# Keys of the second batch turned by a DMA transpose, and their copy moved ahead of two loads

## The chip, the cores and the metric

The kernel runs on one core of a Trainium2 chip. The metric is the device time of one launch in microseconds. A core has five engines that run their own instruction lists: TensorE (matrix multiplies), VectorE, ScalarE, GpSimd (POOL) and SyncE (SP). The last two also start most of the DMA transfers here, GpSimd the loads that change the type from float32 to bfloat16, SyncE the transposes within on-chip memory and the stores of the output. Sixteen DMA engines do the transfers of all queues.

## The reference, cut to what matters

Grouped attention over 8 batches (16 query heads share 4 key and value heads, 384 positions, head size 64), followed by a feed-forward block with a squared ReLU on all 3072 tokens:

```python
scores = scale * np.matmul(q, k.transpose(0, 1, 3, 2))
attn = np.exp(scores - max) ; attn = attn / sum(attn)
x = np.matmul(attn, v)            # heads side by side: 3072 x 1024
h = np.maximum(x @ w_in, 0.0)     # 3072 x 2048
out = h * h @ w_out               # 3072 x 1024, float32
```

Inputs are float32; the kernel computes in bfloat16 with float32 sums.

## The kernel before, in words

The kernel is written through a recorder (`Recorder`). Every operation is added with its engine, the tiles it reads and writes, and a modelled cost. The recorder keeps a modelled clock for each engine and a modelled end of the work in each DMA queue (`ring`), derives the semaphore waits from the reads and writes, and in the end gives each engine its list in the order of adding. Within one engine the order is thus fixed before the launch; a late transfer holds up everything behind the instruction that waits for it.

**Work of one batch.** Keys and queries must lie with the head size across partitions, so they are turned. The keys of a group are first written twice side by side (`dup_k`, line 263) so that two query heads can be scored at once. Then either TensorE turns them by a multiply with the identity into PSUM, from where VectorE copies them to `kT` (`turn_k_pe`, lines 291 and 297, one group of keys, three 128x128 blocks, per call), or one DMA transpose on SyncE's queue turns all four groups at once (`turn_k_dma`, line 272). Queries have the same two ways: `turn_q_pe` (lines 308 and 315, six blocks of one group) and `turn_q_dma` (line 278, half of a batch: two groups, twelve blocks). Scores, exponentials on ScalarE (line 344 for batch 0, 365 later), the multiply with the values (line 380) and the division (395) follow; the attention output is turned into `xT` on TensorE for batch 0 (line 413) and by DMA after that (line 400). The feed-forward block of a batch reads `xT`: sixteen column blocks of the up-projection (line 437, `w_in` in eight slices, two column blocks to a slice), then six output tiles of the down-projection (line 493, sixteen matmuls each, `w_out` in four quarters: two halves of the columns by two halves of the rows).

For batch 0 the down-projection goes through the first column half for its three row tiles, and then the second half the same way; within the first two tiles it does the upper half of the rows of `w_out` for both before the lower half for either.

**Order.** All weight loads, and the loads of batches 0 and 1, are added to GpSimd's list by hand before the planner starts. The planner is the long loop at the end. At each step it collects candidates (score bursts, value multiplies, turns, pieces of the feed-forward block), gives each the modelled time at which its inputs and a PSUM bank are there, and takes the most urgent of those that are ready, or the earliest. `turn_q` is the list of turns for TensorE in batches 0 and 1; a turn of batch 1 may go while fewer than six value pairs of batch 0 are done, or once all of batch 0's `xT` is there. `chores` holds work for GpSimd and SyncE, put into their lists when the planner's clock reaches the modelled end of what they read. From batch 2 on, `prepare` puts there the copy of the keys, one DMA turn for keys, two for queries, and the copy of the values. The loads of batch 2 are added when `turn_q` is empty. Modelled costs of a DMA turn are 1.4 for keys and 2.5 for half the queries, or 8.0 when the modelled load queue still has work at that time; in that case the load queue is made longer by the 1.4 or 2.5.

In the kernel before, batch 0 is turned on TensorE, and of batch 1 four groups of keys and two groups of queries; the other two groups of queries of batch 1 are turned by DMA.

Of the kernel before, what the change touches and what calls it, by code (L numbers as in the profile page):

```python
# [136 lines left out]
def bass_gqa_attention__then__ffn_squared_relu_kernel(  # L137
# [26 lines left out]
    def sb(name, shape, dt=bf16):  # L164
        return nc.alloc_sbuf_tensor(name, shape, dt)

    ident = sb("ident", [128, 128])
    q_st = [sb(f"q_st{i}", [128, H, NJ * D]) for i in range(NST)]
# [3 lines left out]
    k_dup = [sb(f"k_dup{i}", [128, NU, 2, D]) for i in range(2)]  # L172
# [54 lines left out]
    def load_v(b):  # L227
        st = b % NST
        R.add("gpsimd", lambda g: g.dma_start(  # L229
            v_st[st].ap().rearrange("p (g j) d -> p g (j d)", g=HKV),  # L230
            v[b].rearrange("g (p j) d -> p g (j d)", j=NJ)),
            writes=[("v_st", st)], dma=f"v{st}", cost=1.1, issue=0.8)

    def load_q(b, h0, h1):
        st = b % NST
        R.add("gpsimd", lambda g: g.dma_start(  # L236
            q_st[st][:, h0:h1, :],
            q[b, h0:h1].rearrange("h (p j) d -> p h (j d)", j=NJ)),
            writes=[("q_st", st, h // 4, h % 4 // 2) for h in range(h0, h1, 2)], dma=f"q{st}_{h0}",
            cost=0.265 * (h1 - h0), issue=0.8)  # L240
# [4 lines left out]
    def load_w_in(i):  # L245
        R.add("gpsimd", lambda g: g.dma_start(  # L246
            w_in_sb[:, :, i * WC:(i + 1) * WC],
            moe_w_in[:, i * WC:(i + 1) * WC].rearrange("(c p) f -> p c f", p=128)),
            writes=[("w_in", i)], dma=f"wi{i}", cost=2.65, issue=0.9)
# [9 lines left out]
    def dup_k(b, g0=0, g1=HKV):  # L259
        n = (g1 - g0) * NJ  # L260
        src = (k_st[b % NST] if b else k_f32)[:, g0 * NJ:g1 * NJ, :].unsqueeze(2).to_broadcast([128, n, 2, D])
        dst = k_dup[b % 2][:, g0 * NJ:g1 * NJ, :, :]
        R.add("gpsimd", lambda e: e.tensor_copy(dst, src),  # L263
              reads=[("k_st", b % NST) if b else ("k_f32", g) for g in range(g0, g1)],
              writes=[("k_dup", b % 2, g, x) for g in range(g0, g1) for x in range(2)], cost=0.125 * n)
# [5 lines left out]
    def turn_k_dma(b):  # L271
        R.add("sync", lambda e: e.dma_start_transpose(
            out=kT[b % 2].ap(), in_=k_dup[b % 2].ap().rearrange("p n x d -> p (n x d)")),
            reads=[("k_dup", b % 2, g, x) for g in range(HKV) for x in range(2)],
            writes=[("kT", b % 2, g) for g in range(HKV)], dma="turn_k", cost=1.4, shared=8.0)

    def turn_q_dma(b, half):
        R.add("sync", lambda e: e.dma_start_transpose(
            out=qT[b % 2][:, 12 * half:12 * half + 12, :],
            in_=q_st[b % NST][:, 8 * half:8 * half + 8, :].rearrange("p h e -> p (h e)")),  # L280
            reads=[("q_st", b % NST, 2 * half + i, x) for i in range(2) for x in range(2)],
            writes=[("qT", b % 2, 2 * half + i, t) for i in range(2) for t in range(6)], dma=f"turn_q{half}", cost=2.5, shared=8.0)
# [247 lines left out]
    aug_v(0, "gpsimd")  # L530
    load_q(1, 0, 8)
    load_q(1, 8, 16)
    load_w_in(1)
    load_v(1)
    dup_k(1)
    for i in range(2, 6):
        load_w_in(i)
    aug_v(1, "gpsimd")
# [36 lines left out]
    for group in ((0, 1), (2, 3), (4, 5), (6, 7), (8, 9), (10, 11)):  # L575
        if 0 < group[0] < NU - 2:
            smalls += [[(u, 0, 512)] for u in group] + [[(u, 512, 256) for u in group]]
        else:
            smalls += [[(u, c0, 384)] for c0 in (0, 384) for u in group]
    turn_q = [(0, 0, "a"), (0, 0, "c")]  # L580
    turn_q += [(b, g, w) for b in range(2) for g in range(HKV) for w in "kq"
               if (b, g) != (0, 0) and (b, g // 2, w) != (1, 1, "q")]
    sc_q = [(0, n) for n in range(len(smalls))] + [(b, u) for b in range(1, B) for u in range(0, NU, 2)]
    av_q = [(b, c) for b in range(B) for c in range(8)]
    o_q = []
# [1 line left out]
    scored, pairs, turned, up_done = set(), 0, 1, -1  # L587
    x_done = {b: 0 for b in range(B)}
    loaded, queued = 1, 1
    chores = [([("q_st", 1, 2, 0)], lambda: turn_q_dma(1, 1))]  # L590
    turned_g |= {(1, g, t) for g in (2, 3) for t in range(6)}

    def prepare(b):
# [20 lines left out]
    while av_q or av_open or sc_q or o_q or f_head is not None:  # L614
# [18 lines left out]
        if turn_q:  # L633
            b, g, w = turn_q[0]
# [5 lines left out]
        elif av_q:  # L640
            b, c = av_q[0]
# [5 lines left out]
        if sc_q:  # L647
            b, u = sc_q[0]
# [25 lines left out]
        if f_head is not None and not lanes:  # L674
            b, chunks, need, banks, piece = f_head
# [15 lines left out]
        if what[2] == "turn":  # L691
            b, g, w = turn_q.pop(0)
# [5 lines left out]
        elif what[2] == "av":  # L698
            b, c = av_q.pop(0)
            av_open = (b, c, av(b, c, spare))  # L700
            next(av_open[2])
        elif what[2] == "av2":
            b, c, rest = av_open
# [8 lines left out]
        elif what[2] == "o":  # L712
            b, c, _ = o_q.pop(0)
            turn_o_pe(b, c, spare)
            x_done[b] += 1
        elif what[2] == "sc":
            b, u = sc_q.pop(0)
# [44 lines left out]
```

## Time and profile before

| What | Value |
| --- | --- |
| Median of 3 runs (range) | 428.36 us (427.99 to 428.46) |
| Profiled execution: its own time | 427.99 us |
| Its span, first to last instruction | 426.2 us |
| Granted TensorE clock | 1.000 |
| TensorE busy | 419.3 us, 98% of the span |
| TensorE weight loads busy | 231.6 us, 54% |
| VectorE, ScalarE, GpSimd busy | 157.9, 194.7, 55.2 us |
| Moved by DMA | 44.30 MB, mean 104 GB/s |
| Loads started by GpSimd (q0) | 17.44 MB, 32.8% of 16 engines' span |
| Transposes, stores, first loads (q1) | 25.86 MB, 29.3% |

In the rows of the profile, "PE" is TensorE's matmuls, "PEld" its weight loads, "DVE" VectorE, "ACT" ScalarE, "POOL" GpSimd, "SP" SyncE; "POOLq" or "SPq" mark the issue of a transfer. A row of the order in time begins with the start and the length of a group of instructions in us, then engine, line, operation, the output and input tiles and the count; brackets give the time that the engine sat idle ahead of it and what ended that. The matmuls are pipelined and their ends are modelled, so the distances between weight loads say more about TensorE's pace than the matmuls' own durations.

### The profile page before, as it was taken

What the parts mean: (1) busy time and instruction counts of PE and PEld (TensorE: products, weight loads), DVE (VectorE), ACT (ScalarE), POOL (GpSimd) and SP (SyncE); (2) the same over time, 40 slices, a digit from 0 to 9 for tenths busy, and PEclk for the clock granted to TensorE, in tenths of its full rate; (3) what the DMA queues carried; (4) which work ended last, traced back from release to release, by engine and by line L of the source; (5) the groups of instructions that cost most, each with busy time, mean ns of one, the idle gap of its engine ahead of it and who ended that gap; (6) DMA issues with size and microseconds to landing.
All of it is one profiled execution on the core that took longest, in us unless ns stands there. A gap on an engine that the chain in (4) does not pass through costs nothing.

```text
span 426.2 us, 7806 instructions
## 1 busy us (share of the span) xinstructions
PE 419.3 (98%) x3433; PEld 231.6 (54%) x3463; DVE 157.9 (37%) x332; ACT 194.7 (46%) x194; POOL 55.2 (13%) x67
## 2 busy tenths in 40 slices
PE   8999999999999999999999999999999999999997
PEld 5565554565545655455554555545564465446544
DVE  3664431343424443234442344333441244114412
ACT  6957730576246772457735577731240033003300
POOL 8680001414012004004000000000000000000000
PEclk9999999999999999999999999999999999999999
DMA  9999999999699269549919310052001100110012
GB/s 179 192 175 200 186 202 204 225 155 170 103 192 163 31 131 126 123 98 145 105 52 173 88 45 18 2 107 94 25 2 49 74 26 1 51 74 26 1 67 82
DMA packets 96915, 44.30 MB, mean 104 GB/s; under 512 B 77296, under 2 KB 90864, under 8 KB 96880
## 3 DMA queue, kind: packets, MB, share of 16 engines
q0 software_dynamic: 36544, 17.44, 32.8%
q1 hardware_dynamic: 59664, 25.86, 29.3%
q8 instruction: 27, 0.44, 0.4%
q10 hardware_dynamic: 672, 0.49, 0.4%
q14 instruction: 8, 0.07, 0.1%
HBM read 35.65 MB, written 12.58 MB: 113 GB/s over the span
## 4 chain that ended last, share of the span: by engine, by line
PE 96%; POOL 2%; ACT 1%; issue 1%; DVE 0%; POOLq 0%
PE ps L437 40%; PE ps L493 39%; PE ps L380 8%; PE ps L355 7%; ACT expT L344 1%; PE ps L334 1%; POOL q_st L236 1%; PE ps L413 0%; POOL k_dup L263 0%; PE ps L291 0%; POOL w_in_sb L246 0%; POOL v_st L229 0%; POOL k_st L204 0%; PE ps L308 0%; DVE y_sb L502 0%
## 5 line engine op out<-in xcount | busy, mean ns | idle before, releaser
L437 PE MATMUL ps<-xT,w_in_sb 128*128 128x384 bf16 x1024 | 175.0, 326 | 0.0
L493 PE MATMUL ps<-w_out_sb,h2T 128*128 128x512 bf16 (+2 forms) x754 | 166.9, 375 | 2.2 <-issue 1.0
L365 ACT ACTIVATE expT<-ps 128x3072 bf16<-128x3072 f32 x42 | 114.5, 2726 | 63.2 <-PE ps L355 62.6
L437 PEld LDWEIGHTS ps<-xT,w_in_sb 128*128 128x128 bf16 x1024 | 97.1, 98 | 69.6 <-issue 6.2
L447 ACT ACTIVATE h2T<-hr 128x384 bf16<-128x384 f32 x128 | 64.5, 522 | 142.9 <-DVE hr L445 142.9
L493 PEld LDWEIGHTS ps<-w_out_sb,h2T 128*128 128x128 bf16 x784 | 73.7, 98 | 87.2 <-issue 5.1
L445 DVE TENSOR_SCALAR hr<-ps 128x384 f32<-128x384 f32 x128 | 71.3, 558 | 106.5 <-PE ps L437 106.5
L502 DVE COPY y_sb<-ps 128x512 f32<-128x512 f32 (+2 forms) x49 | 33.4, 681 | 123.9 <-PE ps L493 123.9
L380 PEld LDWEIGHTS ps<-v_aug,expT 128*128 128x128 bf16 x1152 | 40.0, 97 | 7.0 <-issue 0.6
L380 PE MATMUL ps<-v_aug,expT 128*128 128x65 bf16 x1152 | 41.9, 193 | 0.0
L395 DVE TENSOR_TENSOR o_sb<-ps,rinv 128x384 bf16<-128x384 f32 x64 | 35.7, 558 | 2.2
L355 PE MATMUL ps<-qT,kT 64*128 64x512 bf16 (+1 forms) x336 | 34.6, 325 | 0.0
L355 PEld LDWEIGHTS ps<-qT,kT 64*128 64x128 bf16 x336 | 13.0, 94 | 20.4 <-issue 6.1
L389 DVE RECIPROCAL rinv<-ps 128x6 f32<-128x6 f32 x64 | 12.2, 190 | 26.2 <-PE ps L380 26.1
L344 ACT ACTIVATE expT<-ps 128x1024 bf16<-128x1024 f32 (+1 forms) x20 | 17.1, 981 | 0.9 <-PE ps L334 0.9
L268 POOL COPY v_aug<-v_st 128x768 bf16<-128x768 bf16 x8 | 6.7, 833 | 83.0 <-PE ps L380 69.6
L263 POOL COPY k_dup<-k_st 128x1536 bf16<-128x1536 bf16 x7 | 10.3, 1469 | 43.1 <-DMA k_st<-in_k_dram 43.0
L236 POOL DMA_DIRECT2D q_st<-in_q_dram x17 | 14.9, 884 | 0.9 <-POOLq L747 0.8
L204 POOL DMA_DIRECT2D k_st<-in_k_dram x7 | 5.3, 760 | 39.2 <-DMA qT<-q_st 39.2
L334 PE MATMUL ps<-qT,kT 64*128 64x384 bf16 (+2 forms) x48 | 7.2, 331 | 0.4 <-DVE qT L315 0.2
L246 POOL DMA_DIRECT2D w_in_sb<-in_moe_w_in_dram x8 | 7.1, 894 | 0.0
L229 POOL DMA_DIRECT2D v_st<-in_v_dram x8 | 6.3, 785 | 0.1
(26 smaller groups left out, 41.0 us busy)
## 6 DMA issues: line engine op xcount, KB each, us to landing
out_dram<-y_sb SPq DMA_DIRECT2D x47, 256.0 KB, 2.0
q_st<-in_q_dram POOLq DMA_DIRECT2D x14, 384.0 KB, 8.9
w_in_sb<-in_moe_w_in_dram POOLq DMA_DIRECT2D x8, 512.0 KB, 15.1
w_out_sb<-in_moe_w_out_dram POOLq DMA_DIRECT2D x4, 1024.0 KB, 31.4
v_st<-in_v_dram POOLq DMA_DIRECT2D x8, 192.0 KB, 10.3
k_st<-in_k_dram POOLq DMA_DIRECT2D x7, 192.0 KB, 4.2
q_st<-in_q_dram POOLq DMA_DIRECT2D x3, 192.0 KB, 5.0
xT<-o_sb SPq DMA_TRANSPOSE x28, 3.0
```

What stands on the lines that cost most here:

```text
L236: R.add("gpsimd", lambda g: g.dma_start(q_st[st][:, h0:h1, :], q[b, h0:h1].rearrange("h (p j) d -> p h (j d)", j=NJ)), writes=[("q_st", st ...
L344: R.add("scalar", lambda e: e.activation(dst, src, AF.Exp, scale=0.125), reads=keys, writes=[("expT", (b * NU + u) % NEX, t) for u, _, _ i ...
L355: m = pe.matmul(flat[:, k0 * HC + c0:k0 * HC + c1], kT[b % 2][64 * x:64 * x + 64, u + k0, :], q_cols(b, (u + k0) // NJ, x, c0, c1))
L365: R.add("scalar", lambda e: e.activation(dst, src, AF.Exp, scale=0.125), reads=keys, writes=[("expT", (n + m) % NEX, t) for m in range(2) ...
L380: m = pe.matmul(po[:, f - 6 * s2, 0:D + 1], w, v_aug[b % 2][:, g * NJ + j, 0:D + 1], start=(j == 0), stop=(j == NJ - 1))
L389: R.add("vector", lambda e: e.reciprocal(rinv[r].ap().unsqueeze(2), po[:, :, D:D + 1]), reads=[("bank", i)], writes=[("rinv", r)], cost=0.13)
L395: R.add("vector", lambda e: e.tensor_tensor(dst, srcv, rbv, ALU.mult), reads=[("bank", i), ("rinv", r)], writes=[("o_sb", o, s2)], cost=0.48)
L437: m = pe.matmul(bank(i)[:, 0:S], w_in_sb[:, kc, c * 128:(c + 1) * 128], xT[b % NXT][:, kc, :], start=(kc == 0), stop=(kc == NKC - 1))
L445: R.add("vector", lambda e: e.tensor_scalar_max(hr[r][:, :], bank(i)[:, 0:S], 0.0), reads=[("bank", i)], writes=[("hr", r)], cost=0.48)
L447: R.add("scalar", lambda e: e.activation(h2T[b % 2][:, c, :], hr[r][:, :], AF.Square), reads=[("hr", r)], writes=[("h2T", b % 2, c)], cost ...
L493: m = pe.matmul(bank(i)[:, 0:n], h2T[b % 2][:, c, i3 * 128:(i3 + 1) * 128], w_out_sb[:, c, c0:c1], start=(c == 0), stop=(c == NFC - 1))
L502: R.add("vector", lambda e: e.tensor_copy(ysl, bank(i)[:, 0:n]), reads=[("bank", i)], writes=[("y", yb)], cost=0.08 + n / 960)
```

## The change

Two edits, both for batch 1. On GpSimd's hand-written list the copy of its keys (`dup_k(1)`) moves from behind the load of `w_in` slice 1 and the load of its values to a place ahead of both. And its four groups of keys leave TensorE's list of turns; instead a chore puts one DMA transpose of all four groups into SyncE's list, ahead of the DMA turn of half its queries. What stays in `turn_q` for batch 1 are the queries of groups 0 and 1.

```diff
     load_q(1, 0, 8)
     load_q(1, 8, 16)
+    dup_k(1)
     load_w_in(1)
     load_v(1)
-    dup_k(1)
     for i in range(2, 6):
         load_w_in(i)
     aug_v(1, "gpsimd")
...
     turn_q = [(0, 0, "a"), (0, 0, "c")]
     turn_q += [(b, g, w) for b in range(2) for g in range(HKV) for w in "kq"
-               if (b, g) != (0, 0) and (b, g // 2, w) != (1, 1, "q")]
+               if (b, g) != (0, 0) and (b == 0 or (g < 2 and w == "q"))]
...
-    chores = [([("q_st", 1, 2, 0)], lambda: turn_q_dma(1, 1))]
+    chores = [([("k_dup", 1, 0, 0)], lambda: turn_k_dma(1)), ([("q_st", 1, 2, 0)], lambda: turn_q_dma(1, 1))]
     turned_g |= {(1, g, t) for g in (2, 3) for t in range(6)}
```

## Prediction

> **What bounds the kernel now.** I read the page first. TensorE is busy for 98% of the span and carries 96% of the chain that ended last, so two things count: TensorE work that leaves the list, and waits that enter it. The 40 slices (10.65 us each) add what the shares hide: for the first ten slices the DMA engines are as full as TensorE. The loads issued at the start last until 74.9 us, when the last of them (values of batch 2, issued at 30.19, 44.7 us to landing) is there.
>
> ```profile
> PE   8999999999999999999999999999999999999997
> PEclk9999999999999999999999999999999999999999
> DMA  9999999999699269549919310052001100110012
> ```
>
> Then I read the instructions in order of time for the first 82 us, where everything that the change touches lies.
>
> ```profile
> 7.44 15.62 ACT L344 ACTIVATE expT<-ps 128x768 bf16<-128x768 f32 x18 [0.38 <-PE ps L334]
> 10.64 0.91 POOL L246 DMA_DIRECT2D w_in_sb<-in_moe_w_in_dram  x1
> 13.91 1.47 POOL L263 COPY k_dup<-k_st 128x1536 bf16<-128x1536 bf16 x1 [1.61 <-DMA k_st<-in_k_dram]
> ...
> 17.88 0.17 PEld L291 LDWEIGHTS ps<-ident,k_dup 128*128 128x128 bf16 x3 [0.23 <-DVE xT L419]
> 18.06 3.62 SPq L278 DMA_TRANSPOSE qT<-q_st  x1
> 19.74 0.17 PEld L291 LDWEIGHTS ps<-ident,k_dup 128*128 128x128 bf16 x3 [0.17 <-issue]
> ...
> 25.14 0.38 PEld L308 LDWEIGHTS ps<-ident,q_st 128*128 128x128 bf16 x6
> 25.48 0.38 PEld L291 LDWEIGHTS ps<-ident,k_dup 128*128 128x128 bf16 x6
> 25.82 2.59 PEld L437 LDWEIGHTS ps<-xT,w_in_sb 128*128 128x128 bf16 x17
> ```
>
> The reader is to see two stages. From 7.4 to 23.1 us ScalarE's exponentials follow each other without a break, and TensorE fills in around them. From 25 us on, the weight loads follow each other closely and TensorE is the bound. The key turns at 17.9 and 19.7 lie in the first stage; the turn of queries (1, group 1) at 25.1 and of the last two key groups at 25.5 lie at the start of the second.
>
> Third, the DMA queues in two stretches: 24.5 to 29 us, when the one DMA turn of batch 1 (half its queries) runs beside the weight loads, and 30 to 39 us, weight loads alone.
>
> ```profile
> q0 software_dynamic: 1088, 0.55, 87.7%
> q1 hardware_dynamic: 1089, 0.28, 46.5%
> ```
>
> ```profile
> q0 software_dynamic: 3498, 1.77, 144.9%
> ```
>
> q0 holds GpSimd's loads, q1 the turn; the first number is packets. Alone, the loads move 3498 packets in 9 us, 389 per us. Beside a turn both move 242 per us, one for one. That is the price list for the change.
>
> Last, how late the weights are. The four quarters of w_out are issued from 24.23 us, and the second view gives the time from issue to landing.
>
> ```profile
> 24.23 3.53 POOL L252 DMA_DIRECT2D w_out_sb<-in_moe_w_out_dram  x4
> DMA to landing us min/median/max: 23.6/31.4/39.7
> 62.11 12.65 PEld L493 LDWEIGHTS ps<-w_out_sb,h2T 128*128 128x128 bf16 x60
> ```
>
> The last quarter is issued at 26.84 and takes 39.7: it lands at 66.5. Its first reader is the 65th weight load of line 493 (three output tiles of 16 and two halves of 8 come before it; 36 are done by 60.8, and up to 67.9 there are 64), at 67.97. Slack: 1.5 us. In the same way the second quarter lands at 54.0 (25.09 + 28.9) and is first read at 55.6, slack 1.6; w_in slice 4 lands at 33.6 (17.06 + 16.5), read from 35.9, slack 2.3. TensorE waits for none of them today, but none is early by much.
>
> **The change, part by part.** *Removed:* 4 groups of keys turned on TensorE, 12 weight loads with 12 matmuls, 0.17 us per group (0.34 for two), 0.69 us together, and 4 VectorE copies of 0.36 us. Two groups lie in ScalarE's stage and by themselves bring nothing. But batch 1's turn list now holds just two query groups. The second was at 25.14, because after six finished pairs the planner holds such turns back until batch 0's x is complete. As next in line it should go at about 19.4, in the second key group's place, beside the exponentials. So the stage where TensorE is the bound loses 0.34 us of queries and 0.34 of keys: 0.7 us. VectorE's copies are covered there; without that cover they would be worth no more than 0.36 each.
>
> *Moved:* the key copy of batch 1 goes ahead of w_in slice 1 and of batch 1's values on GpSimd's queue. The copy still waits for its keys to 13.91 and ends at 15.38. Behind it, slice 1 is issued at 15.4 instead of 10.64, the values at 16.3 instead of 11.51, slices 2 to 5 from 17.1 instead of 15.32. This costs only if the load queue runs dry. It still carries queries until 18.07 (the turn waiting for them is issued at 18.06). A load into an idle queue landed 3.5 us after issue (192 KB of keys at 81.44, about 1 us of data, so first data within some 1.5 to 2 us). Slice 1 can thus start at about 17, as the queries' data ends: a hole of 0 to 0.5 us, and I take 0.2, near the low end because the queue is not idle. The copy of the values and the last loads wait behind the values' landing as before; q0 has slices queued then.
>
> *Added:* one DMA turn on SP's queue, ahead of the query turn. It has the same shape as that one (128 x 1536, 1536 packets). The query turn took 3.62 us on SP and 12.2 us to land; issued at 15.4 the keys land between 15.4 + 6.8 (the later key turn that landed in 6.8) and 27.6. The first scores of batch 1 want them at about 28.0 (28.73 less 0.7): just covered, with nothing to spare if two turns in a row are slower. The query turn behind it lands some 4 us later than its 30.3; its reader is the fourth score burst at 45.7, covered.
>
> The real price is the load queue. 1536 packets at 242 per us take 6.35 us; in that time q0 moves 1536 packets instead of 2470, so every later load lands 2.4 us later. Between 23.4 and 24.3 us, beside the query turn, the DMA rate fell to 9 to 63 GB/s; whether the new turn brings a second such stall (0.9 to 1.0 us) the trace cannot say, so I take half. The delay: 2.4 + 0.2 + 0.5 = 3.1 us, bounds 2.4 and 3.9. The queue stays full until its last landing at 74.9, so nothing gives it back. Nor can it be a gain: no packet is removed.
>
> A rule speaks against the change: the Trainium skill (VectorE: DVE Perf Modes, The three transpose paths, with the rules for kernel authors) would turn 128x128 blocks on TensorE where PSUM will do, giving 390 ns there and 1309 ns for the DMA crossbar. By its figures TensorE would save 12 x 0.39 = 4.7 us, an estimate, and the turn would occupy DMA for 15.7. The trace has 0.057 us per block on TensorE and 0.53 us of shared DMA time, so the saving is far smaller than by the page, and its preference holds all the more.
>
> **The sum.** The saving brings TensorE 0.7 us earlier to weights that come 3.1 us later. The last quarter of w_out lands at 69.6 instead of 66.5, against a first use at 67.97 in the old time: 1.6 us late (bounds 0.9 and 2.4). The waits for slice 4 (3.1 - 2.3 = 0.8) and for the second quarter (1.5) are on the same account, not added. The 0.7 is used up by waiting earlier. Behind 70 us TensorE is dense, so the lateness stays to the end. The profiled execution took 427.99 us (span 426.2 and 1.8 around it), so it would take 429.6; it lies 0.37 below the median of 428.36, on which the forecast stands: 428.36 + 1.6 = 430.0 us. Because the delayed tail of w_out now also meets the first two output stores (64.5 to 67 us, where q0 fell to 0.18 MB in 2.5 us), up to 0.5 more is possible: the likeliest case runs from 429.2 to 431.3.
>
> **The rivals.** *The delay is hidden* (it ends on the other side or level): if the turn costs q0 less than 1.5 us, all weights are in time and only the 0.7 remains: 428.36 - 0.7 = 427.7. For it: the uncovered key turns later in the span land in 3.9 us. Against: that is with q0 idle. It decides at a delay of 1.5 us.
>
> *A real gain:* the list is planned anew, and waits before weight loads of 0.2 to 0.3 us around 17 to 29 us go as well. Three or four would make 1 us, and with the 0.7 and weights in time: 426.7. For it: these waits exist. Against: most stand in ScalarE's stage, and the weights must be in time too.
>
> *Batch 2 waits:* its first scores run at 80.38, and the first query turn they need (issued at 73.37, 6.3 us) lands at 79.7. If they keep their place they are late by 3.1 - 0.7 = 2.4: 430.8, up to 431.6. Against it: I carried the planner's own clock on by hand. It adds 1.4 for the new turn and 0.16 for the moved copy to its model of the loads, which then end at 71.2, past the start of batch 2's key turn (69.9), so that turn is charged 8.0 instead of 1.4, and these scores move about 6 us down the list. A late first key turn (28.0) would cost 0 to 2 us, not on top.
>
> **How the numbers follow.** Late weights 0.60, most of it above 429.2; hidden 0.20; a real gain 0.12; batch 2 or the first keys late 0.08. What a measurement of this kernel can tell is about 0.2%, 0.86 us: faster means under 427.5, slower over 429.2. Faster: the real gain and a little of the hidden case, 0.14. Same: the rest of hidden and the low end of late weights, 0.22. Slower: 0.64. The range cuts the real gain and the far end of the slow cases: 427.4 to 431.4.
>
> **What would show it.** No line 291 for batch 1; a second query group before 23 us; a key turn on SP at 15.4; slice 1 issued at 15.4; all w_out quarters landing 2.4 to 3.9 us after issue plus the old times; TensorE weight loads of lines 437 and 493 with waits near 35, 55 and 68 us that were not there. I am wrong if w_out's last quarter lands before 68, or if TensorE passes 75 us earlier than before.

## The result and the profile after

The changed kernel takes 432.78 us (median of 6 runs, 431.81 to 433.69) against 428.40 us for the kernel before (6 runs, 427.99 to 428.49). The ratio is 1.0102, with a 95% interval of 1.0085 to 1.0119: the change costs 4.4 us. The profiled execution took 433.39 us, with a span of 431.6 us against 426.2. It lies 0.6 us above its median and the one before lay 0.4 below, so the two profiles differ by 1 us more than the medians do. One run of a later experiment, half the move, came at a granted clock of 0.852 with 485.26 us and is left out there.

The page of the kernel after, in the same three parts as before: the slices (10.8 us each), the chain that ended last, and the two groups that wait.

```profile
PE   8979988999999999999999999999999999999997
PEclk9999999999999999999999999999999999999999
DMA  9999999999929908974974810142101200110012
...
PE 82%; DMA 14%; POOL 3%; issue 1%; DVE 0%; POOLq 0%
...
L437 PE MATMUL ps<-xT,w_in_sb 128*128 128x384 bf16 x1024 | 175.3, 326 | 2.3 <-DMA w_in_sb<-in_moe_w_in_dram 2.3
L493 PE MATMUL ps<-w_out_sb,h2T 128*128 128x512 bf16 (+2 forms) x756 | 168.4, 375 | 4.6 <-DMA w_out_sb<-in_moe_w_out_dram 2.8
```

TensorE is still busy for 98% of the span at the full clock, so the shares of busy time hide the loss. The chain shows it: before, TensorE carried 96% of it, now 82%, and DMA 14%. Followed back from the end, the chain stays on TensorE down to the last quarter of w_out and then passes into the transfers. The two groups name what was waited for: w_in and w_out.

The order in time of the kernel after, all engines:

```profile
14.01 1.47 POOL L263 COPY k_dup<-k_st 128x1536 bf16<-128x1536 bf16 x1 [3.35 <-DMA k_st<-in_k_dram]
15.41 0.88 POOL L246 DMA_DIRECT2D w_in_sb<-in_moe_w_in_dram  x1
15.50 2.19 SPq L272 DMA_TRANSPOSE kT<-k_dup  x1
...
18.05 0.67 PEld L308 LDWEIGHTS ps<-ident,q_st 128*128 128x128 bf16 x12 [0.23 <-DVE xT L419]
...
18.94 4.52 SPq L278 DMA_TRANSPOSE qT<-q_st  x1
...
26.25 2.23 PEld L437 LDWEIGHTS ps<-xT,w_in_sb 128*128 128x128 bf16 x15 [0.65 <-DMA w_in_sb<-in_moe_w_in_dram]
...
28.05 0.83 POOL L268 COPY v_aug<-v_st 128x768 bf16<-128x768 bf16 x1 [7.50 <-DMA v_st<-in_v_dram]
```

The keys turn and slice 1 are issued at 15.5 and 15.4 us. Both query groups of TensorE go together at 18.05, and no key group of batch 1 is left on it. GpSimd then stands for 7.5 us in front of the copy of the values.

TensorE's weight loads alone, later in the same order in time; the bracket gives the wait ahead of the group and what ended it:

```profile
28.80 0.44 PEld L355 LDWEIGHTS ps<-qT,kT 64*128 64x128 bf16 x8 [0.32 <-DVE hr L445]
...
32.26 2.39 PEld L437 LDWEIGHTS ps<-xT,w_in_sb 128*128 128x128 bf16 x16 [2.43 <-DMA w_in_sb<-in_moe_w_in_dram]
...
59.41 0.55 PEld L493 LDWEIGHTS ps<-w_out_sb,h2T 128*128 128x128 bf16 x4 [1.61 <-DMA w_out_sb<-in_moe_w_out_dram]
...
73.59 6.37 PEld L493 LDWEIGHTS ps<-w_out_sb,h2T 128*128 128x128 bf16 x31 [2.15 <-DMA w_out_sb<-in_moe_w_out_dram]
```

Against the same events before, TensorE's place is:

| Event on TensorE | before | after | later by | new wait ahead |
| --- | --- | --- | --- | --- |
| first scores of batch 1 | 28.72 | 28.80 | 0.1 | 0.65 (slice 1, at 26.25) |
| first read of w_in slice 2 | 29.82 | 32.26 | 2.4 | 2.43 |
| second quarter of w_out | 55.62 | 59.41 | 3.8 | 1.61 |
| last quarter of w_out | 67.97 | 73.59 | 5.6 | 2.15 |
| end of the span | 426.2 | 431.6 | 5.4 | |

So the loss is made before 74 us, in four waits of 6.8 us together. The saving is in it too: ahead of 28.8 us there is a new wait of 0.65, and yet TensorE is only 0.1 later there, so some 0.6 was gained.

Where the loads land, before and after:

| Load | before | after | later by |
| --- | --- | --- | --- |
| w_in slice 1 | 20.6 | 26.2 | 5.6 |
| w_in slice 2 | 26.5 | 32.2 | 5.7 |
| w_in slice 6 | 38.5 | 42.8 | 4.3 |
| last quarter of w_out | 66.5 | 73.6 | 7.1 |
| keys of batch 2 | 69.4 | 75.7 | 6.3 |

The issue of the four quarters of w_out in GpSimd's order in time, kernel after:

```profile
30.56 3.53 POOL L252 DMA_DIRECT2D w_out_sb<-in_moe_w_out_dram  x4
```

And their time from issue to landing, from the view of that tile:

```profile
DMA to landing us min/median/max: 22.5/30.8/40.4
```

They are issued 6.3 us later than before (24.23), because GpSimd issues them behind the copy that waited for the values, and then take about as long.

### The profile page after: what moved, and what is told of

Its sections match the earlier page's. It is cut to its first block, busy times and chain, and to the rows that moved or that the text cites. A ratio compares the mean times of both kernels' runs of the same rounds, so it can differ in the third digit from the quotient of the medians.

```text
span 431.6 us, 7784 instructions
## 1 busy us (share of the span) xinstructions
PE 420.9 (98%) x3423; PEld 231.0 (54%) x3451; DVE 156.8 (36%) x328; ACT 195.7 (45%) x194; POOL 55.2 (13%) x67
## 4 chain that ended last, share of the span: by engine, by line
PE 82%; DMA 14%; POOL 3%; issue 1%; DVE 0%; POOLq 0%
PE ps L493 35%; PE ps L437 34%; DMA w_out_sb<-in_moe_w_out_dram 9%; PE ps L355 6%; PE ps L380 6%; DMA v_st<-in_v_dram 3%; DMA k_st<-in_k_dram 2%; POOL w_in_sb L246 1%; POOL w_out_sb L252 1%; POOL q_st L236 1%; POOL k_dup L263 0%; POOL v_aug L268 0%; POOL v_st L229 0%; DVE y_sb L502 0%; POOL ident L520 0%
## 6 DMA issues: line engine op xcount, KB each, us to landing
w_in_sb<-in_moe_w_in_dram POOLq DMA_DIRECT2D x8, 512.0 KB, 15.5
```

## The experiments

I had one theory and two rivals. *The turn's packets*: the added DMA turn delays the saturated load queue, and this is nearly all of the loss. *The move*: the copy of the keys, put ahead of two loads, leaves the load queue empty for a while. *TensorE's order*: the list without the key turns is planned anew and is itself slower. Every ratio below is to the kernel before in the same set of runs, whose medians were 427.97 to 428.11 us.

**The move alone.** Keys stay on TensorE, whose list is the same as before.

```diff
     load_q(1, 8, 16)
+    dup_k(1)
     load_w_in(1)
     load_v(1)
-    dup_k(1)
```

> Only the copy of batch 1's keys is moved ahead of w_in slice 1 and the values; keys stay on TensorE, whose list is unchanged. Theory A (the DMA turn itself starves the load queue): the move costs a hole of 0 to 0.5 us in the load queue, all of it inside the 1.5 us of slack, so 428.2 to 428.6, the same as before, and no wait of TensorE for weights. Theory B (the late issue of slice 1 starves the load queue between 17 and 20 us): slice 1 lands 2 to 3 us after its old 20.6, the last w_out quarter near 68.5 to 69.5, and the time is 428.9 to 430.

Measured: 429.00 us, ratio 1.0022 (1.0010 to 1.0034). Between 16 and 20 us the queue of the loads (packets, MB, share) moved this in the kernel before:

```profile
q0 software_dynamic: 1731, 0.78, 150.7%
```

And this in the same stretch with the move alone:

```profile
q0 software_dynamic: 1245, 0.56, 118.7%
```

At 433 packets per us the 486 missing ones are a hole of 1.1 us. Slice 1 was issued at 15.53; the thinnest stretch, 17 to 18 us, has 171 packets against 409 before, and the full rate is back at about 18.4. TensorE's waits for w_out (total, times, longest) came with it:

```profile
PEld ps L493 <- DMA w_out_sb<-in_moe_w_out_dram: 1.9, 2, 1.0
```

The move by itself costs about 0.9 us, the low end of theory B. The hole is real, and larger than the 0 to 0.5 us that the prediction allowed. The last quarter of w_out landed at 69.8, 3.3 us later than before, which is more than the hole alone; where the rest comes from is taken up further down, for the whole change.

**The turn alone.** The copy stays where it was; TensorE's list is that of the changed kernel.

```diff
-               if (b, g) != (0, 0) and (b, g // 2, w) != (1, 1, "q")]
+               if (b, g) != (0, 0) and (b == 0 or (g < 2 and w == "q"))]
...
-    chores = [([("q_st", 1, 2, 0)], lambda: turn_q_dma(1, 1))]
+    chores = [([("k_dup", 1, 0, 0)], lambda: turn_k_dma(1)), ([("q_st", 1, 2, 0)], lambda: turn_q_dma(1, 1))]
```

> The keys of batch 1 are turned by DMA, but the copy stays behind slice 1 and the values on GpSimd's list; TensorE's list is that of the changed kernel. Theory A: nearly all of the loss is here, 431.5 to 433, with the thin stretch of the load queue at 17 to 20 us as in the changed kernel. Theory B: no thin stretch; the turn costs its 2.4 us in packets and half a stall, less the slack of 1.5 us: 429.3 to 430.5.

Measured: 431.64 us, ratio 1.0075 (1.0058 to 1.0092). There is no hole at 17 us, the last quarter of w_out lands at 71.7 (5.2 later) and the keys of batch 2 at 73.7 (4.3 later). So neither theory holds as it was written: the time is that of A, the missing hole that of B. The two long waits are for w_out:

```profile
PEld ps L493 <- DMA w_out_sb<-in_moe_w_out_dram: 3.8, 2, 1.9
```

Two shorter waits of 0.7 us are put down to other things, but end at 33.30 and 51.63, as w_in slice 3 (33.2) and the first quarter of w_out (51.5) land. The two halves of the change add up: 0.9 and 3.5 us, 4.4 together, which is what both cost at once.

**A turn that nobody reads, added to the kernel before.** TensorE's list and its savings stay as before, so only the DMA work differs.

```diff
+    kX = sb("kX", [128, NU, 128])
...
+    def turn_extra(b):
+        R.add("sync", lambda e: e.dma_start_transpose(
+            out=kX.ap(), in_=k_dup[b % 2].ap().rearrange("p n x d -> p (n x d)")),
+            reads=[("k_dup", b % 2, g, x) for g in range(HKV) for x in range(2)],
+            writes=["kX"], dma="turn_x", cost=0.0)
...
-    chores = [([("q_st", 1, 2, 0)], lambda: turn_q_dma(1, 1))]
+    chores = [([("k_dup", 1, 0, 0)], lambda: turn_extra(1)), ([("q_st", 1, 2, 0)], lambda: turn_q_dma(1, 1))]
```

> The kernel before with one more DMA turn of batch 1's keys into a tile that nobody reads, at the place where the changed kernel has its turn; the copy is not moved and TensorE's list is unchanged. It measures the price of the turn alone, without the 0.7 us saved on TensorE. Theory A: thin stretch, last w_out quarter 5 to 7 us later, 431.5 to 433. Theory B: 2.4 to 3.4 us later, 429.3 to 430.5.

Measured: 431.32 us, ratio 1.0071 (1.0050 to 1.0091). The last quarter, issued at 28.43, lands at 71.1 (4.6 later), the keys of batch 2 at 73.0 (3.6 later). In this kernel line 493 has moved to 500:

```profile
PEld ps L500 <- DMA w_out_sb<-in_moe_w_out_dram: 2.8, 2, 1.7
DMA to landing us min/median/max: 26.1/33.8/42.7
```

This is the main verdict: with TensorE's list untouched, one more turn beside the loads costs 3.2 us. TensorE's new order isn't needed for the loss. The time lies between the ranges of the two theories, and there is no thin stretch at 17 us; but a second stall came with the turn. From 32 to 34 us all queues moved this, with under 30 GB/s for 0.8 us of it:

```profile
DMA packets 545, 0.23 MB, mean 113 GB/s; under 512 B 176, under 2 KB 545, under 8 KB 545
```

**Two such turns.**

```diff
-    chores = [([("q_st", 1, 2, 0)], lambda: turn_q_dma(1, 1))]
+    chores = [([("k_dup", 1, 0, 0)], lambda: turn_extra(1)), ([("k_dup", 1, 0, 0)], lambda: turn_extra(1)), ([("q_st", 1, 2, 0)], lambda: turn_q_dma(1, 1))]
```

> The kernel before with two further DMA turns of batch 1's keys, one behind the other, into a tile that nobody reads. Theory A (each turn takes its packets from the load queue): another 2.4 us on the 431.3 of one extra turn, 433.5 to 434.5, keys of batch 2 landing near 75.5 instead of 73.0. Theory B (the cost comes once, with the first turn that meets the loads): 431 to 431.7.

Measured: 434.07 us, ratio 1.0137 (1.0121 to 1.0154), 2.75 us above one extra turn. The keys of batch 2 land at 76.1, again 3.1 later. That is theory A: the price is close to linear, and there is no sign that the queue gives anything back.

**The same turn in batch 4**, at a place where the load queue is nearly empty.

```diff
+        if b == 4:
+            chores.append(([("k_dup", b % 2, 0, 0)], lambda: turn_extra(b)))
         chores.append(([("v_st", b % NST)], lambda: aug_v(b, "gpsimd")))
```

> The kernel before with one more DMA turn of keys into a tile that nobody reads, but in batch 4, when the first loads have long landed. Theory A (the price is paid through the load queue alone): nothing, 428.0 to 428.4. Theory B (a turn costs by itself, through SyncE's queue or what waits behind it): 1 us or more, over 429.1.

Measured: 427.95 us, ratio 0.9998 (0.9988 to 1.0008). The turn is issued at 122.58 us and lands 4.1 us later; from 122 to 128 us the load queue moves 23 packets. There a turn costs nothing that can be measured. The price belongs to the loads beside it, not to the turn.

**Keys of batch 1 turned by nobody.** The scores of batch 1 read batch 0's turned keys; TensorE has the saving, DMA no new work.

```diff
-        return [("kT", b % 2, g)] + [("qT", b % 2, g, t) for t in range(c0 // 128, (c0 + n) // 128)]
+        return [("kT", 0 if b == 1 else b % 2, g)] + [("qT", b % 2, g, t) for t in range(c0 // 128, (c0 + n) // 128)]
...
-                                      kT[b % 2][64 * x:64 * x + 64, u + k0, :],
+                                      kT[0 if b == 1 else b % 2][64 * x:64 * x + 64, u + k0, :],
...
-               if (b, g) != (0, 0) and (b, g // 2, w) != (1, 1, "q")]
+               if (b, g) != (0, 0) and (b == 0 or (g < 2 and w == "q"))]
```

> Batch 1's keys are turned by nobody: its scores read batch 0's turned keys instead, so the output of batch 1 is another one. It leaves TensorE's saving and none of the DMA. Both theories: 0.7 us faster than before, 427.5 to 427.9. If the saving is hidden by ScalarE's stage or eaten by the new order: 428.4.

Measured: 428.22 us, ratio 0.9998 (0.9988 to 1.0008). The expected gain didn't appear: TensorE waits 1.0 us for the last quarter of w_out, which lands at 68.3, and 0.5 us for the queries of batch 2.

```profile
PEld ps L493 <- DMA w_out_sb<-in_moe_w_out_dram: 1.0, 1, 1.0
PEld ps L355 <- DMA qT<-q_st: 0.5, 1, 0.5
```

So TensorE's 0.7 us is lost even with no new turn: the quarter was 1.5 us early, TensorE comes 0.7 earlier, and the quarter lands 1.8 later than before, which leaves the 1.0 us of wait. Its landing thus differs by some 2 us between kernels with the same load list. The list of loads is the same, but not what runs beside it: TensorE's new order has a third output store issued at 65.14, ahead of that landing, where before the third came at 72.46. What that store alone is worth was not separated.

**No DMA turn at all in batch 1.** As in the run above, and the queries of groups 2 and 3 are batch 0's too, so the query turn on SyncE goes as well.

```diff
-        flat = qT[b % 2][64 * x:64 * x + 64, 6 * g:6 * g + 6, :].rearrange("p n c -> p (n c)")
+        flat = qT[0 if b == 1 and g > 1 else b % 2][64 * x:64 * x + 64, 6 * g:6 * g + 6, :].rearrange("p n c -> p (n c)")
...
-    chores = [([("q_st", 1, 2, 0)], lambda: turn_q_dma(1, 1))]
+    chores = []
```

> Batch 1 has no DMA turn at all and no key turns on TensorE: its scores read batch 0's turned keys, and for groups 2 and 3 batch 0's turned queries, so the output of batch 1 is another one. Theory A (weights late in the load queue hid the 0.7 us that TensorE saves): the loads land 2.4 us or more before those of the kernel before, TensorE waits for no weight, and the saving shows: 427.3 to 427.7. Theory B (the saving lies beside ScalarE's stage and never counts): 428.0 to 428.4, with no waits for weights either.

Measured: 427.65 us, ratio 0.9988 (0.9979 to 0.9998). The last quarter of w_out lands at 63.8, no weight is waited for, and 0.3 us of the 0.7 shows in the medians (0.5 by the ratio, with 0.1 to 0.9 in its interval), as theory A has it. The saving of the change is real when the loads are early enough, and it is small.

Between 23.3 and 25.1 us, all DMA queues together moved this in the kernel before:

```profile
DMA packets 474, 0.18 MB, mean 98 GB/s; under 512 B 248, under 2 KB 474, under 8 KB 474
```

In the same stretch of the kernel after:

```profile
DMA packets 338, 0.11 MB, mean 61 GB/s; under 512 B 297, under 2 KB 338, under 8 KB 338
```

And with no DMA turn in batch 1:

```profile
DMA packets 682, 0.35 MB, mean 193 GB/s; under 512 B 5, under 2 KB 682, under 8 KB 682
```

The stall of nearly a microsecond that the kernel before has at 23.4 us goes away with the turn (its packets, of 256 bytes, are nearly all of those "under 512 B").

**All turns of batch 1 on TensorE**, the opposite of the change:

```diff
-               if (b, g) != (0, 0) and (b, g // 2, w) != (1, 1, "q")]
+               if (b, g) != (0, 0)]
...
-    chores = [([("q_st", 1, 2, 0)], lambda: turn_q_dma(1, 1))]
-    turned_g |= {(1, g, t) for g in (2, 3) for t in range(6)}
+    chores = []
...
-        if turn_q and (b == 0 or pairs < 6 or x_done[0] == 8) and (sc_q[0] != (0, 0) or w in "ka"):
+        if turn_q and (sc_q[0] != (0, 0) or w in "ka"):
```

> The opposite of the change: all turns of batch 1, its queries of groups 2 and 3 too, on TensorE, with no DMA turn before batch 2, and no holding back after six finished pairs. Theory A: TensorE has 0.7 us more to do in the stage where it is the bound and the loads are early enough: 428.6 to 429.1. Theory B (the kernel before already waits for late weights in its usual runs): the earlier loads pay for the turns, 427.9 to 428.4.

Measured: 428.90 us, ratio 1.0019 (1.0009 to 1.0028). The quarters of w_out land at 43.5, 50.6, 56.9 and 62.1, 3.0 to 4.4 us earlier than before, with no wait for weights. It still isn't faster: no weight was late before either, and TensorE now does 12 more blocks, which at 0.057 us each is 0.7 of the 0.9 us lost (0.8 by the ratio). The kernel before stands between the two, with its loads just early enough.

**Half the move.** The copy goes behind the load of slice 1, ahead of the values; keys stay on TensorE.

```diff
     load_w_in(1)
-    load_v(1)
     dup_k(1)
+    load_v(1)
```

> The copy of batch 1's keys goes ahead of the values but stays behind w_in slice 1; keys stay on TensorE with its list unchanged. Theory A (the move costs because slice 1 is issued when the load queue is nearly dry): no thin stretch at 17 to 18 us, last w_out quarter near 66.5 as before, 427.9 to 428.4. Theory B (any wait of GpSimd in that place, or the values being late, costs): 428.7 to 429.3, as for the full move.

Measured: 428.31 us, ratio 1.0000 (0.9985 to 1.0015). The stretch from 17 to 18 us has 413 packets, as before (409), and the last quarter lands at 67.0. With slice 1 queued ahead of the copy there is no hole, and no cost shows; the interval still allows 0.6 us.

**Half the move with the DMA turn**, twice; the second time beside the changed kernel as it is, on the same chip. The edit is the one above with that of the turn alone.

> The same half move together with the DMA turn of the keys, so the changed kernel without the late slice 1. Theory A: the price of the turn alone, as with the copy unmoved, 431.3 to 431.9. Theory B: the 432.8 of the changed kernel.

Measured: 432.65 us, ratio 1.0095 (1.0063 to 1.0127). This was inconclusive: the interval holds both what the full change costs and what the turn alone does.

> The half move with the DMA turn once more, in more rounds and beside the changed kernel on one chip. Theory A (the late slice 1 is what the full move costs): 431.3 to 432.0, 0.8 us or more under the changed kernel. Theory B (the wait of GpSimd and the late values cost as much): within 0.4 us of the changed kernel.

> The changed kernel once more, as the other half of the comparison: 432.8 us as measured, with the load queue thin from 16.6 to 20 us.

Measured: 432.12 us, ratio 1.0092 (1.0077 to 1.0108), against 433.20 us, 1.0128 (1.0105 to 1.0151), for the changed kernel. The medians are 1.1 us apart, as the hole would have it, but the intervals touch, with 4 and 5 runs that each spread over more than 1.5 us. The profiles don't help. With half the move and the turn, in an execution of 433.39 us:

```profile
PEld ps L493 <- DMA w_out_sb<-in_moe_w_out_dram: 4.2, 2, 2.2
PEld ps L437 <- DMA w_in_sb<-in_moe_w_in_dram: 0.7, 1, 0.7
PEld ps L437 <- issue: 2.7, 6, 1.3
```

For the changed kernel in this set, in an execution of 432.87 us:

```profile
PEld ps L493 <- DMA w_out_sb<-in_moe_w_out_dram: 3.9, 2, 2.0
PEld ps L437 <- DMA w_in_sb<-in_moe_w_in_dram: 1.9, 1, 1.9
PEld ps L437 <- issue: 1.7, 6, 0.3
```

The wait for w_in looks 1.2 us shorter where slice 1 goes out ahead of the copy. But the longest wait of the first "issue" row, 1.3 us, ends at 35.07, as slice 3 lands (35.0), and the weight loads behind it are the first to read that slice: it is in all likelihood a wait for w_in too, and then both kernels waited some 2 us for it. That the late slice 1 is what the full move costs on top of the turn is thus not shown. It is shown for the move without the turn, where the full move costs 0.9 us and half of it nothing that can be seen.

## Why the prediction was right and wrong

The mechanism held and its size did not: 430.0 us was forecast, with a range up to 431.4, and 432.8 came.

**TensorE's saving of 0.7 us: right, as far as it can be seen.** The second query group went at 18.05 beside the exponentials. About 0.6 shows ahead of the first scores, and 0.3 to 0.5 in the time without DMA turns.

**The keys land in time: right.** Issued at 15.50, they landed at 26.1, inside the 22.2 to 27.6 of the prediction and ahead of the scores at 28.80.

**Batch 2 doesn't wait: right.** Its first scores moved from 80.38 down the list to 92.95 (5.6 us of this is the lateness itself), and among TensorE's waits there is none for turned keys or queries of batch 2.

**The turn's packets delay the load queue by 2.4 us: consistent, and only a part of the price.** The two queues move equal numbers of packets in the kernel after too (500 and 499 from 26 to 28 us). This agrees with what the Trainium skill says of arbitration (DMA: Bandwidth & Descriptors, section Queues, rings and completion order): each DMA engine takes turns between queues packet by packet. But an unread turn delayed the keys of batch 2 by 3.6 us and a second one by 3.1, so one turn costs the queue some 3 us or more, with the stall that it brings.

**The delay of 3.1 us (2.4 to 3.9): this is the step that failed.** The last quarter came 7.1 us later in the profiled execution (6.6 in the second profile of the changed kernel, 73.1 against 66.5). The terms beside the packets were mis-sized, each too low:

- The hole of "0 to 0.5, I take 0.2" measured 1.1 us with the move alone. The prediction let the queries' data last until they landed, at 18.07, and slice 1's data start 1.5 to 2 us after its issue; its own row (3.5 us to landing, 1 us of it data) allows 2.5. With the move alone the rate began to fall at 16.5 us, 2 us ahead of the queries' landing (18.5), was a third of before's from 17 to 18, and was full again at 18.4, 2.9 us after the issue.
- The stalls, "up to 1.0, I take half". The time lost in a stretch is its length times the missing share of the rate. Before: 1.8 us at 98 instead of 193 GB/s (23.3 to 25.1 us) and 1.4 at 104 instead of 195 (45.8 to 47.2), 1.5 us in all. After: 1.8 at 61 instead of 193 (23.3 to 25.1), 1.8 at 69 instead of 195 (49.8 to 51.6) and 1.0 at 42 instead of 217 (64.2 to 65.2), 3.2 us in all. The excess is 1.7.
- The output stores, "up to 0.5", kept out of the 3.1 and only in the range. A quarter that comes late meets traffic of the next stage: the last one now also meets a third store, issued at 69.24; before, the next one after the first two came at 72.46, when the quarter had landed. From 68 to 71 us in the kernel after:

```profile
q0 software_dynamic: 310, 0.32, 62.0%
q1 hardware_dynamic: 318, 0.52, 53.8%
```

The loads moved 0.32 MB there, where alone they would move about 0.59. How much the three terms are worth together can be counted. From 10 us to the landing of the last quarter all queues moved 10.97 MB at a mean of 194 GB/s before, and 11.72 MB at 184 GB/s after. The 0.75 MB more are worth 3.9 us at 194 GB/s: 0.39 MB are the keys' turn (2.0 us, where the count of packets gave 2.4), 0.27 MB are output stores and turns of the attention output that before came behind the quarter (1.4 us), and 0.09 MB are later loads (0.5 us). The lower rate makes the other 3.2 us: 1.5 from 16 to 20 us (123 GB/s against 195) and the 1.7 of the stalls. These are estimates from one pair of profiles. A second pair with the same two orders (the turn in batch 4, which runs like the kernel before up to there, and the changed kernel once more) has the quarter 6.3 us later: 4.7 us by more bytes (10.90 and 11.80 MB) and 1.6 by a lower rate (192 and 187 GB/s). So the stalls' share differs between executions, and the extra traffic is there in both.

**From late weights to the end: the prediction's way of reckoning held.** The last quarter's slack was 1.5 us and it came 7.1 late: 5.6 us, and that is by how much its first reader moved (67.97 to 73.59). The end moved by 5.4 in the profiled execution and by 4.4 in the medians. The prediction's 1.6 us came from the same subtraction with 3.1. That the side came out right isn't luck: it needs only a delay beyond 1.5 us, which even the lower bound of 2.4 exceeds.

**Which wait comes first: missed.** The prediction looked for waits near 35, 55 and 68 us. They came at 26, 32, 59 and 74. With slice 1 landing at 26.2 instead of 20.6, slices 1 and 2 were the first to be late. The prediction had checked slack only from slice 4 on, though it was slice 1 that the edit moved.

**What was read too lightly in the code.** The prediction said that the copy of the values and the last loads wait "as before". They did, but the values landed at 28.0 instead of 21.7, so GpSimd issued slice 6 at 28.82 and w_out from 30.56. The queue still had work at that time, so this wait cost nothing that the trace shows; it had used up the lead of the issue, though.

**The hidden delay and the real gain, as rivals,** fell: both needed weights in time. The unread turn shows a delay far above the 1.5 us from which they are late.

## What to carry to other kernels

When the loads at the start saturate the DMA engines and arrive only 1 or 2 us before they are read, work added beside them is paid at the end as far as it goes beyond that lead: here a turn of 12 blocks that nobody read cost 3.2 us, against the 0.7 us of TensorE's work that the change saves, while the same turn beside a nearly empty load queue cost nothing. Before moving an operation ahead of a load on an in-order queue, work out when that load can start and reach its full rate, and check the slack of that very load first. To price a transfer beside others, count its packets one for one, add the stalls that such transfers show elsewhere in the same trace as a whole, not by half, and count the traffic of the next stage that a late load will then meet.

## What the runs showed of the hardware

- Loads and DMA turns together can stall. The stretch of 0.8 to 0.9 us near 24 us at 6 to 40 GB/s is there in the kernel before and with an extra turn, and it is gone in the two kernels without a DMA turn in that place (193 and 197 GB/s between 23.3 and 25.1 us). Here is the other one, all turns of batch 1 on TensorE:

```profile
DMA packets 702, 0.35 MB, mean 197 GB/s; under 512 B 9, under 2 KB 702, under 8 KB 702
```

  What causes the stall, and why it is longer in the kernel after, stays open. Its length differs between executions: near 47 us the rate was under 50 GB/s for 0.5 us in the kernel before and for 1.1 us in the run with the turn in batch 4, whose order is the same up to there.
- A load issued into a queue that is running empty takes long to fill it: with the move alone, slice 1 was issued at 15.53 and the full rate was back at about 18.4 us. With slice 1 queued ahead of the copy the thin stretch is not there (413 packets from 17 to 18 us against 171).
- Between kernels with the same load list, the landing of the last quarter of w_out moved by up to 2 us: 66.5 us before, 67.0 with half the move, 68.3 with the keys turned by nobody. In the last one a third store was issued ahead of the landing (65.14 instead of 72.46). What each difference is worth was not isolated.
